# RWKV attention and a SiLU feed-forward on one core: the first chunk in pairs of neighbouring tokens, two batches per tile, its bonus summed on TensorE

## The chip, the cores and the metric

The kernel runs on 1 core of a Trainium2 chip. The metric is the device time of one execution in microseconds (us), lower is better. The kernel before has a median of 195.09 us over 3 runs (194.4, 195.09 and 197.38). About 2% is what a measurement of this kernel can tell from no change.

## What is computed

An RWKV-style linear attention with a per-channel decay, then a feed-forward layer with SiLU. Batch 4, 8 heads, 768 tokens, head size 48; model width 384, inner width 2048; 3072 tokens in all. Inputs and output are float32.

```python
def _attn_ref(r, k, v, w, u):
    state = np.zeros((B, H, D, D))
    for t in range(S):
        kt, vt, rt = k[:, :, t], v[:, :, t], r[:, :, t]
        cur = einsum('bhd,bhe->bhde', u[None] * kt, vt)
        y[:, :, t] = einsum('bhd,bhde->bhe', rt, state + cur)
        state = w[None, :, :, None] * state + einsum('bhd,bhe->bhde', kt, vt)

def _moe_ref(x, w_in, w_out):      # x: y with the heads side by side, 3072 x 384
    h = x @ w_in
    return (h * (1 / (1 + exp(-h)))) @ w_out
```

The term with `u` is the bonus: the token's own value, weighted by the sum over a head's channels of r * u * k.

## The kernel before

**Units and chunks.** Tokens are cut into 6 chunks of 128 (`C`). A unit is one chunk of one batch, so there are 24 units; unit i is chunk i // 4 of batch i % 4. Units 0 to 3 are the first chunk, which has no state coming in and whose decay runs over all 128 tokens. Later chunks are worked off in halves of 64 tokens (`HC`) and in pairs of batches.

**One unit of the first chunk.** r, k and v come in by one DMA each (`ld`, L72), one token per partition, so each contiguous piece is one token of one head, 48 floats or 192 bytes. In SBUF a head of r and k has 64 columns, of which 16 are zero. TensorE turns r and k (`turn_one`, L261): 8 transposes each, one for each pair of heads and each half of 64 tokens. All of them have 64 rows and 112 columns; the page writes such a shape as 64*112. VectorE multiplies what comes out by powers of w (`decay_one`, L269) into rT and kT. TensorE forms the products k.r of all pairs of tokens (`product_pair`, L295), VectorE masks them (`masked`, L302), TensorE multiplies them with v in half precision (`outputs_y`, L312), and VectorE adds the bonus while it copies the result out (`evict_y`, L317). Three transposes (`turn_y`, L469) and a copy on ScalarE (`copy_x`, L473) make it the input xT of the feed-forward. GpSimd does the bonus: k*u (L221), times r (L225); VectorE sums each head (L234); GpSimd multiplies v by that sum (`vu`, L239). GpSimd also makes the decayed k (`kc`, L229), from which `first_sums` (L326) and `first_state` (L337, L342) make the state that goes into the second chunk.

**The feed-forward.** `l1_mm` (L484) multiplies xT with 128 or 256 columns of `w_in` into PSUM, `l1_silu` (L492) applies SiLU on ScalarE, `l2_mm` (L505) multiplies with `w_out`, and `store` (L511 to L515) writes out. The weights come in by GpSimd's queue in four pieces each (`ld_win` L83, `ld_wout` L88), and are cast to half precision on the way.

**What sets the order.** Nothing is scheduled by a planner: each engine runs its instructions in the order in which the program emits them. From the first chunk to the middle of the second this order is a list of words written out by hand (`order`, L584 to L595). `T0` is the turning of unit 0, `rT0` its decay, `A01` the products of units 0 and 1, `am0` the mask, `Y0` the outputs, `y160` the bonus and copy, `yT0` and `xT0` the way to the feed-forward, `S0` and `st0` the states of units 0 and 1; `L0.4` and `G0.4` are `l1_mm` and `l1_silu` for the first two batches and columns 4 and 5 of 16, `L2.x` the same for the other two batches; `i_q1` asks for the second quarter of `w_in`. `4*` ahead of a word puts four 128x512 matmuls on zeros before it (`spin`, L166). `lnwb` and `lamC` (`powers_c`, L193 to L201) make the powers of w on ScalarE and load the SiLU table; `pads` (L160) zeroes the unused columns of eight input tiles on ScalarE. The PSUM tiles `att` alternate between two buffers; all others share four (tag "moe").

**Queues.** SyncE issues almost all loads; ScalarE issues the load of k for unit 0, of `u_bc` and of `w_row`. From `L2.0` on (L589) the order is the same in both kernels, but for the places of the two pair-wise steps named below.

Of the kernel before, what the change touches and what calls it, by code (L numbers as in the profile page):

```python
# [8 lines left out]
FP = mybir.dt.float32  # L9
# [6 lines left out]
def kernel(  # L16
# [11 lines left out]
    nc = tc.nc  # L28
# [33 lines left out]
    rin = [big.tile([128, H, 64], FP, name=f"rin{i}") for i in range(NIN)]  # L62
    kin = [big.tile([128, H, 64], FP, name=f"kin{i}") for i in range(NIN)]
    vin = [big.tile([128, H, D], FP, name=f"vin{i}") for i in range(NIN)]
    kc = [big.tile([128, H, 64], F16, name=f"kc{i}") for i in range(NIN)]
    st = [big.tile([PR, 2, NP, D], FP, name=f"st{b}") for b in range(B // 2)]
    win = big.tile([128, NQ, DFF], F16)
    wout = big.tile([128, NFT, HD], F16)

    def ld(i, dst, src, eng=nc.sync):  # L70
        sc, b = unit(i)
        eng.dma_start(  # L72
            out=dst[i % NIN][:, :, 0:D],
            in_=src[b, :, sc * C:sc * C + C, :].rearrange("h t d -> t h d"))

# [16 lines left out]
    def columns(eng, dst, src, j):  # L92
# [8 lines left out]
    nc.vector.memset(idle, 0.0)  # L101
    columns(nc.sync, wpT, w, 1)
    columns(nc.scalar, wpT, w, 0)
    nc.scalar.dma_start(out=w_row, in_=bass.AP(tensor=w.tensor, offset=0, ap=[[0, 1], [1, HD]]))
    ld(0, rin, r)
    ld(0, kin, k, nc.scalar)
    nc.scalar.dma_start(out=u_bc, in_=bass.AP(tensor=u.tensor, offset=0,
                                              ap=[[0, 128], [D, H], [1, D]]))
    ld(1, rin, r)
    ld(1, kin, k)  # L110
    ld(0, vin, v)
    ld(1, vin, v)
    load(2)
    load(3)
    nc.vector.memset(ones, 1.0)
    for i in range(B):
        nc.vector.memset(rin[i][:, :, D:64], 0.0)
        nc.vector.memset(kin[i][:, :, D:64], 0.0)
# [6 lines left out]
    it_rev = cst.tile([128, 1], FP)  # L125
    nc.gpsimd.iota(it_rev, pattern=[[0, 1]], base=C - 1, channel_multiplier=-1,
                   allow_small_or_imprecise_dtypes=True)
    it_half = cst.tile([128, 1], FP)
    for y in range(2):
        nc.gpsimd.iota(it_half[HC * y:HC * y + HC], pattern=[[0, 1]], base=HC - 1,  # L130
                       channel_multiplier=-1, allow_small_or_imprecise_dtypes=True)
    maskM = cst.tile([128, C], FP)
    nc.gpsimd.memset(maskM, 1.0)
    nc.gpsimd.affine_select(
        out=maskM, in_=maskM, compare_op=ALU.is_ge, fill=0.0,
        base=-1, channel_multiplier=-1, pattern=[[1, C]])
    ident16 = cst.tile([128, 128], F16)
    nc.gpsimd.tensor_copy(out=ident16, in_=ident)
    maskX = cst.tile([128, C], FP)
    maskH = cst.tile([128, HC], FP)  # L140
# [4 lines left out]
    for i in range(NIN):  # L145
        nc.gpsimd.memset(kc[i][:, :, D:64], 0.0)
# [6 lines left out]
    lamC = cst.tile([128, H, D], FP)  # L153
# [41 lines left out]
    def powers_c():  # L195
        nc.scalar.activation(out=lamC.rearrange("p h d -> p (h d)"), in_=lnw_bc,
                             func=AF.Exp, scale=it_rev)
# [4 lines left out]

    def cross_mask():
        nc.scalar.copy(out=maskX[0:HC, :], in_=maskM[HC:C, :])
        nc.scalar.copy(out=maskX[HC:C, :], in_=maskM[0:HC, :])
        for y in range(2):
            nc.scalar.copy(out=maskH[HC * y:HC * y + HC, :],
                           in_=maskM[HC * y:HC * y + HC, HC * y:HC * y + HC])
# [19 lines left out]
    def decayed_k(i):  # L228
        nc.gpsimd.tensor_tensor(out=kc[i % NIN][:, :, 0:D], in0=kin[i % NIN][:, :, 0:D],  # L229
                                in1=lamH if unit(i)[0] else lamC, op=ALU.mult)  # L230
# [33 lines left out]
    def decay_one(i, x):  # L264
        key, lam = (("rT", lamR), ("kT", lamK))[x]
        L(i)[key] = wrk.tile([PR, NP, C], FP, name=key)
        lam = (lam[:, :, 0:HC].unsqueeze(1).broadcast_to([PR, 2, NP, HC]) if unit(i)[0]
               else lam.rearrange("p g (y t) -> p y g t", y=2))
# [16 lines left out]
    def product_pair(i):  # L285
        a = [next_att().rearrange("p j (g c) -> p j g c", g=NP) for _ in range(2)]
        for e in range(2):
            L(i + e)["a"] = a[e]
# [397 lines left out]
```

## Time and profile before

One profiled execution took 194.21 us, with a span of 192.5 us; the remaining 1.7 us lie around the span.

| engine | busy, share of the span | busy from 0 to 25.48 us | busy from 50 us on (142.5 us) |
|---|---|---|---|
| TensorE (PE) | 180.4 us, 94% | 21.03 us | 136.99 us |
| VectorE (DVE) | 107.7 us, 56% | 18.15 us | 72.06 us |
| ScalarE (ACT) | 118.5 us, 62% | 17.03 us | 81.83 us |
| GpSimd (POOL) | 117.2 us, 61% | 20.76 us | 74.79 us |

25.48 us is where the first matmul of `L2.0` starts, the first step from which both kernels run the same list. The sixteen DMA engines are fully used in the first 50 us and at about half after that. Granted TensorE clock: 1.00 throughout. A profile's row of the timeline reads: start, length, engine, line, operation, written tile <- read tiles, shape (for TensorE: rows*columns of the stationary operand, then the moving one), how often, and in brackets the idle time ahead of it with what ended it. Rows of equal instructions in a run are merged; the length is from the start of the first to the end of the last.

### The profile page before, as it was taken

How to read it: one execution, taken by the hardware profiler on the slowest of the kernel's cores; microseconds unless marked ns; L12 is line 12 of the kernel's file. 1: busy time of each engine (PE TensorE's matmuls, PEld its weight loads, DVE VectorE, ACT ScalarE, POOL GpSimd, SP SyncE). 2: the span in 40 equal slices, each digit the busy share in tenths (PEclk: the TensorE clock that was granted, in tenths of full speed). 3: DMA queues.
4: the chain of work that ended last, by engine and by line, in shares of the span. 5: the costliest groups of instructions: out<-in, count | busy, mean ns of one | idle time of the engine just before them, and what ended most of it. 6: DMA issues, size and time to landing. Idle time of an engine off the chain costs nothing. (4 is left out here: it accounts for less than half of the span.)

```text
span 192.5 us, 6544 instructions
## 1 busy us (share of the span) xinstructions
PE 180.4 (94%) x2786; PEld 112.2 (58%) x2786; DVE 107.7 (56%) x183; ACT 118.5 (62%) x235; POOL 117.2 (61%) x151
## 2 busy tenths in 40 slices
PE   7888898989999999999999999999999999899993
PEld 2455684567756876745546646557656456444562
DVE  7578775846965846836827826917924914200120
ACT  5499478779383495198593297683397773189200
POOL 6499999599899955949659459469339320000000
PEclk9999999999999999999999999999999999999999
DMA  5999999999268568278185286294286201210022
GB/s 94 215 214 198 208 200 184 159 224 217 33 117 166 184 138 169 80 149 202 29 169 136 72 178 168 46 191 125 55 166 170 41 23 66 71 52 0 2 83 83
DMA packets 90272, 24.42 MB, mean 127 GB/s; under 512 B 83329, under 2 KB 90242, under 8 KB 90242
## 3 DMA queue, kind: packets, MB, share of 16 engines
q1 hardware_dynamic: 84992, 20.39, 48.4%
q0 software_dynamic: 3712, 3.15, 10.8%
q10 hardware_dynamic: 1538, 0.46, 1.1%
q8 instruction: 22, 0.36, 0.8%
q14 instruction: 8, 0.07, 0.1%
HBM read 20.65 MB, written 4.72 MB: 132 GB/s over the span
## 5 line engine op out<-in xcount | busy, mean ns | idle before, releaser
L484 PE MATMUL hps<-xT,win 128*128 128x512 f16 (+1 forms) x360 | 66.4, 337 | 1.0 <-DMA xT<-y 0.9
L492 ACT ACTIVATE gT<-hps 128x512 f16<-128x512 f32 x96 | 55.3, 600 | 16.6 <-PE hps L484 14.1
L505 PE MATMUL ops<-wout,gT 128*128 128x384 f16 x368 | 63.0, 326 | 1.3 <-ACT gT L492 1.3
L505 PEld LDWEIGHTS <-gT 128*128 128x128 f16 x368 | 34.9, 98 | 25.4 <-ACT gT L492 2.5
L484 PEld LDWEIGHTS <-win 128*128 128x128 f16 x360 | 33.6, 98 | 26.9 <-issue 2.1
L221 POOL TENSOR_TENSOR ku<-kin,u_bc 128x384 f32<-128x384 f32 x24 | 24.7, 1029 | 15.0 <-DMA kin<-in_k_dram 11.7
L239 POOL TENSOR_TENSOR vu<-vin,rku 128x384 f32<-128x384 f32 x24 | 19.8, 837 | 19.1 <-DVE rku L234 19.1
L511 ACT COPY osb<-ops 128x384 f32<-128x384 f32 x20 | 9.6, 478 | 30.7 <-PE ops L505 27.9
L448 DVE TENSOR_TENSOR y<-yp,vu 64x384 f16<-64x384 f32 x40 | 21.3, 554 | 11.8 <-PE yp L437 5.7
L225 POOL TENSOR_TENSOR rku_f<-rin,ku 128x384 f32<-128x384 f32 x24 | 24.5, 1020 | 1.7
L392 DVE TENSOR_TENSOR s<-sp,sdec 112x384 f32<-112x384 f32 x10 | 5.6, 558 | 32.9 <-PE sp L379 30.9
L229 POOL TENSOR_TENSOR kc<-kin,lamH 128x384 f16<-128x384 f32 x20 | 20.7, 1036 | 0.0
L269 DVE TENSOR_TENSOR kT<-att,lamK 112x512 f32<-112x512 f32 x24 | 16.3, 677 | 4.7 <-PE att L261 4.7
L269 DVE TENSOR_TENSOR rT<-att,lamR 112x512 f32<-112x512 f32 x24 | 16.2, 677 | 2.3 <-PE att L261 2.3
L337 ACT CAST s1h<-s 48x384 f16<-48x384 f32 x20 | 10.2, 510 | 6.5 <-DVE s L392 6.2
L248 ACT CAST v<-vin 128x384 f16<-128x384 f32 x24 | 11.5, 510 | 2.7 <-DMA vin<-in_v_dram 2.5
L513 DVE COPY osb<-ops 128x384 f32<-128x384 f32 x3 | 1.7, 558 | 20.5 <-issue 16.4
L234 DVE TENSOR_REDUCE rku<-rku_f 128x8 f32<-128x384 f32 x24 | 12.4, 538 | 1.0 <-POOL rku_f L225 1.0
L363 DVE TENSOR_TENSOR am<-att,maskH 128x1024 f16<-128x1024 f32 x10 | 12.2, 1218 | 1.3 <-PE att L356 1.3
L283 ACT CAST rT<-rT 112x512 f16<-112x512 f32 x20 | 12.4, 620 | 0.1
L356 PE MATMUL att<-rT,kT 48*64 48x64 f32 x640 | 11.6, 220 | 0.0
L356 PEld LDWEIGHTS att<-rT,kT 48*64 48x64 f32 x640 | 10.4, 135 | 0.0
(81 smaller groups left out, 183.8 us busy)
## 6 DMA issues: line engine op xcount, KB each, us to landing
rin<-in_r_dram SPq DMA_DIRECT2D x24, 192.0 KB, 3.6
vin<-in_v_dram SPq DMA_DIRECT2D x24, 192.0 KB, 4.7
kin<-in_k_dram SPq DMA_DIRECT2D x23, 192.0 KB, 4.7
out_dram<-osb SPq DMA_DIRECT2D x23, 192.0 KB, 3.2
win<-in_moe_w_in_dram POOLq DMA_DIRECT2D x4, 384.0 KB, 6.0
wout<-in_moe_w_out_dram POOLq DMA_DIRECT2D x4, 384.0 KB, 6.4
xT<-y SPq DMA_TRANSPOSE x18, 2.3
kin<-in_k_dram ACTq DMA_DIRECT2D x1, 192.0 KB, 3.8
```

The costliest lines, as they stand in the source:

```text
L221: nc.gpsimd.tensor_tensor(out=L(i)["ku"], in0=kin[i % NIN][:, :, 0:D], in1=u_bc, op=ALU.mult)
L225: nc.gpsimd.tensor_tensor(out=L(i)["rku_f"], in0=rin[i % NIN][:, :, 0:D], in1=L(i)["ku"], op=ALU.mult)
L229: nc.gpsimd.tensor_tensor(out=kc[i % NIN][:, :, 0:D], in0=kin[i % NIN][:, :, 0:D], in1=lamH if unit(i)[0] else lamC, op=ALU.mult)
L234: nc.vector.tensor_reduce(out=L(i)["rku"], in_=L(i)["rku_f"], axis=mybir.AxisListType.X, op=ALU.add)
L239: nc.gpsimd.tensor_tensor(out=L(i)["vu"], in0=vin[i % NIN], in1=L(i)["rku"].unsqueeze(2).broadcast_to([128, H, D]), op=ALU.mult)
L269: nc.vector.tensor_tensor(out=L(i)[key].rearrange("p g (y t) -> p y g t", y=2), in0=L(i)["t"][0:PR, :, x], in1=lam, op=ALU.mult)
L283: nc.scalar.copy(out=L(i)["rT16"], in_=L(i)["rT"])
L356: nc.tensor.matmul(a[o0:o0 + HC, j, e, p, :], kT[r0:r0 + D, p, HC * x:HC * x + HC], rT[r0:r0 + D, p, HC * x:HC * x + HC], start=True, stop ...
L448: nc.vector.tensor_tensor(out=L(i + e)["y16"][rows].rearrange("p h d -> p (h d)"), in0=L(i)["y2"][r][rows, 0:HD], in1=L(i + e)["vu"][rows] ...
L484: nc.tensor.matmul(hps[:, f, :], win[:, q, (ft + f) * 128:(ft + f + 1) * 128], xts[sc][:, q, b0:b0 + nb, :].rearrange("p b t -> p (b t)"), ...
L492: nc.scalar.activation(out=gts[sc][:, ft:ft + m, b0 * C:(b0 + nb) * C], in_=hpss[b0, ft], func=AF.Silu)
L505: nc.tensor.matmul(opss[b], gts[sc][:, ft, b * C:(b + 1) * C], wout[:, ft, :], start=(ft == 0), stop=(ft == NFT - 1))
```

## The change

Only the first chunk (units 0 to 3) is done in another way. Two batches become a pair (g = 0, 1); e names the batch in the pair, j the parity of a token.

- **Loads.** `ldX` puts batch 2g on partitions 0 to 63 and batch 2g+1 on 64 to 127. A partition holds tokens 2p and 2p+1, next to each other, so that a contiguous piece has 384 bytes. One DMA fills 64 partitions; there are as many DMAs as before and half as many pieces. A head now takes 112 columns (`DP`): 96 of data and 16 of padding. ScalarE issues both loads of k for pair 0 before `w_row`, and two small loads of u, transposed; `u_bc` moves to SyncE, behind the loads of pair 1.
- **Turning.** `turn_x` does one head at a time and one parity: for each pair of heads, first two transposes of 64*112 for the odd head, then two of 64*64 for the even one (each for the two batches). That is 32 for r and 32 for k of a pair of batches, where there were 16 and 16. In the program a 64*112 transpose has the tile size 64x128, a 64*64 one has 64x64.
- **Products by parity.** `product_x` does for each parity of k the two parities of r, 64x64 each; `masked_x` masks; `outputs_x` sums over the parity of k in PSUM, 64 small matmuls for a pair of batches.
- **Bonus.** GpSimd multiplies the decayed rT and kT (`bonus_x`); eight float32 matmuls with the factors u*w (`usel`) sum the heads on TensorE (`bonus_sum_x`); ScalarE copies the 16 sums per row (`bonus_out_x`); GpSimd multiplies v by them, as before. Per unit, two GpSimd products and a VectorE sum become one GpSimd product.
- **The rest.** The decayed k of a pair is one GpSimd instruction on 768 columns, and needs the powers `lamX` (two instructions in place of `lamC`). The masks are made on GpSimd; `cross_mask` and the two swapped copies of v go for the first chunk. The state is made in six smaller copies per pair in place of three (`state_x`).
- **The order.** The list is written anew up to `L2.0`. Of what follows, only `x.S.1` and `x.st.1` stand where `S2` and `st2` stood, and the steps `kc2`, `kc3` and `i_q3` are elsewhere.

```diff
+    def ldX(g, dst, src, eng=nc.sync):
+        for e in range(2):
+            o = dst[g][HC * e:HC * e + HC]
+            o = o.rearrange("p h j d -> p h (j d)") if dst is vX else o[:, :, 0:2 * D]
+            eng.dma_start(out=o, in_=src[2 * g + e, :, 0:C, :].rearrange(
+                "h (p j) d -> p h (j d)", j=2))
...
     columns(nc.sync, wpT, w, 1)
     columns(nc.scalar, wpT, w, 0)
+    ldX(0, rX, r)
+    ldX(0, kX, k, nc.scalar)
     nc.scalar.dma_start(out=w_row, in_=bass.AP(tensor=w.tensor, offset=0, ap=[[0, 1], [1, HD]]))
...
-    load(2)
-    load(3)
+    ldX(0, vX, v)
+    columns(nc.scalar, uT, u, 0)
+    columns(nc.scalar, uT, u, 1)
+    ldX(1, rX, r)
+    ldX(1, kX, k)
+    ldX(1, vX, v)
...
     def powers_c():
-        nc.scalar.activation(out=lamC.rearrange("p h d -> p (h d)"), in_=lnw_bc,
-                             func=AF.Exp, scale=it_rev)
+        for j in range(2):
+            nc.scalar.activation(out=lamX[:, :, j, :],
+                                 in_=lnw_bc.rearrange("p (h d) -> p h d", h=H),
+                                 func=AF.Exp, scale=it_two[:, j:j + 1])
...
+    def turn_x(g, x):
+        t = X(g)["t", x] = next_att().rearrange("p e (j g t) -> p e j g t", j=2, g=NP)
+        src = (rX, kX)[x][g].rearrange("p h x -> p (h x)")
+        for j in range(2):
+            for p in range(NP):
+                for h, p0, n in ((2 * p + 1, 64, PR), (2 * p, 0, 64)):
+                    for e in range(2):
+                        rows = slice(HC * e, HC * e + HC)
+                        c0 = DP * h + D * j - p0
+                        nc.tensor.transpose(t[0:n, e, j, p, :], src[rows, c0:c0 + n],
+                                            ident[rows, rows])
...
+    def bonus_sum_x(g):
+        bk = X(g)["bk"] = ps.tile([128, 512], FP, name="bk", tag="moe", bufs=4)
+        for j in range(2):
+            for p in range(NP):
+                c0 = 2 * (NP * j + p)
+                nc.tensor.matmul(bk[:, c0:c0 + 2], X(g)["q", j][:, p, :], usel[:, p, :],
+                                 start=True, stop=True)
...
     order = """
-        lnw eK lamK mx clear lr4 lk4 lv4 lr5 lk5 lv5 lr6 lk6 lv6 lr7 lk7 lv7 4*T0 ku0 rT0 kT0
-        4*T1 rT1 kT1 v160 ru0 rd0 ku1 wb v161 A01 ru1 am0 rd1 vu0 lnwb i_q0 lamC pads am1 vu1
-        4*Y0 y160 T2 kT2 2*Y1 y161 ku2 ru2 rT2 yT0 xT0 i_q1 yT1 xT1 v162 T3 kT3 rT3 ku3 ru3 rd2
-        v163 4*A23 vu2 i_q2 rd3 vu3 am2 am3 L0.0 G0.0 L0.2 G0.2 Y2 y162 Y3 y163 kc0 yT2 xT2 L0.4
-        G0.4 kc1 yT3 xT3 L0.6 G0.6 S0 st0 kc2 T4 kT4 rT4 kc3 L2.0 G2.0 L2.2 G2.2 ku4 v164
-        L2.4 G2.4 S2 L2.6 G2.6 st2 ru4 i_q3 r164 L4.8 G4.8 L4.9 G4.9 rd4 ku5 kc4 kc5 sd4
+        lnw eK lamK us clear lr4 lk4 lv4 lr5 lk5 lv5 lr6 lk6 lv6 lr7 lk7 lv7
+        4*x.t.0.0 x.d.0.0.0 x.d.0.0.1 x.t.0.1 x.d.0.1.0 x.d.0.1.1 x.q.0.0 x.q.0.1 i_q0
+        2*wb lnwb x.P.0.0 x.P.0.1 x.m.0.0 x.m.0.1 lamX x.v16.0 pads x.B.0 x.rk.0 x.vu.0.0 x.vu.0.1 i_q1
+        x.t.1.0 x.d.1.0.0 x.d.1.0.1 x.t.1.1 x.d.1.1.0 x.d.1.1.1 2*x.Y.0 x.e.0.0 x.e.0.1
+        x.q.1.0 x.q.1.1 i_q2 2*x.yT.0 x.xT.0.0 x.xT.0.1 x.P.1.0 x.m.1.0 x.P.1.1 x.m.1.1 x.v16.1
+        L0.0 G0.0 L0.2 G0.2 x.B.1 x.rk.1 x.vu.1.0 x.vu.1.1 L0.4 G0.4 x.kc.0 i_q3 x.Y.1 x.e.1.0 x.e.1.1
+        L0.6 G0.6 x.yT.1 x.xT.1.0 x.xT.1.1 x.S.0 x.st.0 x.kc.1 T4 kT4 rT4
+        L2.0 G2.0 L2.2 G2.2 ku4 v164 L2.4 G2.4 x.S.1 L2.6 G2.6 x.st.1 ru4 r164 L4.8 G4.8 L4.9 G4.9
```

In the new words, `x.t.g.0` turns r of pair g and `x.t.g.1` its k; `x.d` are the decays, `x.q` the GpSimd products for the bonus, `x.B` their sums on TensorE, `x.rk` the copy of the sums, `x.vu` v times the sums, `x.P` the products, `x.m` the masks, `x.Y` the outputs, `x.e` the bonus and copy, `x.yT` and `x.xT` the way to the feed-forward, `x.kc` the decayed k, `x.S` and `x.st` the state.

## The prediction

> **What bounds the kernel now.** I read the page's first two parts, then busy time by stage, then the timelines of TensorE and ScalarE up to 26 us, then DMA. The first view is the page; the second gives busy time in three stages (length, then each engine, then clock, DMA share, GB/s).
>
> ```profile
> PE 180.4 (94%) x2786; PEld 112.2 (58%) x2786; DVE 107.7 (56%) x183; ACT 118.5 (62%) x235; POOL 117.2 (61%) x151
> ...
> DMA  5999999999268568278185286294286201210022
> ```
> ```profile
> 0.00:25.48 25.48, 21.03 (x316) 12.88 (x317) 18.15 (x38) 17.03 (x40) 20.76 (x41) 1.00 1.02 188
> 25.48:50.00 24.52, 22.36 (x450) 15.58 (x450) 17.48 (x30) 19.68 (x38) 21.65 (x25) 1.00 1.09 186
> 50.00:192.50 142.50, 136.99 (x2044) 83.74 (x2036) 72.06 (x117) 81.83 (x157) 74.79 (x86) 1.00 0.46 106
> ```
>
> From 50 us on TensorE is busy for 136.99 of 142.5 us: nothing done earlier elsewhere shortens that. The change edits only what stands ahead of the first matmul of L2.0. So the question is one number: when does L2.0 start, now 25.48 us? The list behind it is the same, so a delay there passes to the end nearly one for one. From 25.48 to 50 us TensorE idles 24.52 - 22.36 = 2.2 us, mostly behind engines fed by TensorE itself, so I let that move along and absorb nothing.
>
> TensorE's timeline around a turn (line 261) shows what a new shape of the array costs; the last line, from the tile's own view, has min/median/max ns of one transpose:
>
> ```profile
> 12.86 0.37 PE L312 MATMUL yp<-v,am 128*128 128x48 f16 x8 [0.36 <-DVE am L302]
> 13.16 0.44 PE L261 MATMUL att<-ident,rin 64*112 64x64 f32 x8
> 13.43 0.39 PE L261 MATMUL att<-ident,kin 64*112 64x64 f32 x8
> 13.75 0.60 PE L166 MATMUL zs<-idle 128*128 128x512 f16 x2
> ...
> 25.48 2.14 PE L484 MATMUL hps<-xT,win 128*128 128x256 f16 x18
> ```
> ```profile
> L261 PE MATMUL att<-ident,kin x48: 216/216/269, 5.9 to 31.1; 64*112 64x64 f32 x48
> ```
>
> Eight transposes run as four pairs (two row halves at once). In the second run the last pair starts 0.39 - 0.216 = 0.17 us after the first: 0.058 a pair, 0.23 for four. But the first run takes 0.27 until the second starts, so entering the shape cost 0.04, and the second takes 0.32 until the spin starts, so leaving cost 0.09. A change of shape is 0.13 us, over twice the pair itself. Before, a unit pays it once for 16 transposes.
>
> ScalarE's timeline has the chain that the new bonus must go through; DMA's has two stretches of the SyncE queue (packets, MB, share of sixteen engines), from 10 to 12 us with 192-byte pieces, and from 63 to 64 us almost all 1536-byte rows:
>
> ```profile
> 11.45 0.49 ACT L193 ACTIVATE lnw_bc<-bc 128x384 f32<-128x384 f32 x1
> 11.97 0.61 ACT L196 ACTIVATE lamC<-lnw_bc,it_rev 128x384 f32<-128x384 f32 x1
> 12.49 0.60 ACT L198 ACTIVATE lamH<-lnw_bc,it_half 128x384 f32<-128x384 f32 x1
> 13.00 0.19 ACT L200 ACTIVATE wHT<-lnwT 112x4 f32<-112x4 f32 x1
> 13.20 1.28 ACT L201 ACT_TABLE_LOAD   x1
> 14.50 0.30 ACT L160 CAST rin<-idle 128x128 f32<-128x128 f16 x1
> ```
> ```profile
> q1 hardware_dynamic: 2229, 0.42, 107.3%
> ```
> ```profile
> q1 hardware_dynamic: 301, 0.39, 105.4%
> ```
>
> **Part 1, loads (gain).** 1.073 x 16 x 2 us / 2229 = 15.4 ns for 192 bytes. In the other stretch 50 of the 301 packets are under 512 bytes and nearly free, so 1.054 x 16 us / 251 = 67 ns for 1536. The straight line gives 23 ns for 384 bytes, against 31 for two of 192. Before, the second k landed when its transposes began, at 8.15 us. Now pair 0 needs r and k, 128 packets an engine, 2.9 us; the first r load before landed 3.0 us after its issue at 1.43, of which 1.0 was its own 64 packets, so the flow counts from about 3.2 and pair 0 is there at 5.9 to 6.1 us; I take 5.9. The two added loads of u on ScalarE cost its queue 0.43 us each, and delay the powers of w (3.26 us now) by one to two us; the first decay comes after 9, which hides it.
>
> **Part 2, turning (loss).** `turn_x` alternates 64*112 and 64*64 pairs, 16 pairs a call. If every pair pays the change, one costs 0.058 + 0.13 = 0.19 to 0.2 us, so a call lasts 3.2 us against 16 x 0.058 = 0.93. Bounds: 0.058 (the change of width is free; below that nothing speaks for a gain) and 0.266 a pair (each waits for all of the one before, the longest record). I take 0.2, because changes of shape cost about that everywhere in this timeline. [...]
>
> **Part 3, the chain with these prices (us).** TensorE: r of pair 0 5.9 to 9.1, its k to 12.3. VectorE's two k decays (0.6 each) end at 13.1 and 13.75. TensorE: two spins 0.5 and `wb` 0.85, to 13.65 (row of before: 8.52 to 9.36); products 2 x 0.55 to 14.75 (64 of this shape take 1.16 at 33.34). GpSimd: `q` twice from 13.1; 384 columns take 1.0, so 512 take 1.3: 15.7, then `i_q0` 0.8. ScalarE from 13.75: 0.5 + 3 x 0.52 + 0.2 + 1.3 for `lnwb`, powers and table, two casts 1.0, eight pads 0.2 each, together 6.15 = 19.9; only then, in its own order, the copy of the bonus sums, 20.1. `vu` twice (0.82) on GpSimd ends at 21.75, and `i_q1`, queued behind it, is issued there; it took 6.0 to land, so 27.75.
>
> TensorE meanwhile: bonus sums 15.7 to 16.4 (8 float32 matmuls; bounds 0.3 by the transposes' rate and 1.1 by a 0.13 us weight load each; both stay inside waits), then, in order ahead of `x.Y.0`, the two turns of pair 1: 16.4 to 22.8. Spins 0.5, outputs 0.6: 23.9. VectorE: last decays of pair 1 to 24.15, `x.e` to 25.25. TensorE: y transposes to 25.65, products of pair 1 to 26.75; ScalarE's two copies 26.7; L0.0 and L0.2 at 0.75 each, 28.25; sums 28.95; L0.4 (weights there) 29.7; `x.Y.1` 30.3. The bonus of pair 1: ScalarE copy 29.25, `vu` twice 30.95; `x.e.1.1` 31.5; transposes 31.9; ScalarE 32.9; GpSimd's `x.kc.0` (768 columns, 1.9) ends at 32.85; state matmuls 33.35; T4 33.9. So L2.0 starts at 33.9 instead of 25.48: 8.4 us late.
>
> GpSimd drops about 2.7 us of chunk-0 work (3.8 a unit now; then 1.3 + 0.82 + 0.95), and the swapped copies (2.0 us on ScalarE), mask copies and four VectorE sums (2.2) go. I cost these at nothing: all three engines wait for TensorE here. The six state copies (0.36 against 0.56 for half the columns) lie beside L2.x.
>
> **Sum:** 194.2 (profiled execution) + 8.4 = 202.6 us. The median of before stands 0.9 above the profiled execution; I keep the latter. The 2% (what a measurement can tell) end at 191.2 and 199.0.
>
> [...]
>
> **The rivals.**
> - *The change of width is free; not slower.* At 0.058 a pair: r and k turned at 7.8, `wb` 9.15, copy of the sums after ScalarE's 6.15 at 15.6, `vu` 17.25, `i_q1` lands at 23.25, L0.4 24.0, `x.Y.1` 24.6, `x.e` 25.75, ScalarE 27.05, L2.0 27.4: +1.9, 196.1 us, no change. For it: no row of before alternates 64*112 with 64*64. Against it: every other change of shape in the timeline leaves such a gap. It decides from about 0.08 us a change down (a pair at 0.13 gives +4.7).
> - *The loads win.* Pair 0 is there 2.2 us earlier, and nothing behind it takes longer: 192 us. Against it, ScalarE's order puts table and pads ahead of the copy.
> - *The clock drops as well.* Spins step by 0.48 us in the first 5 us (4 in 1.9) and by 0.26 later (4 in 1.04). If the long stretches of tiny matmuls count as idle, two turns at half speed add 2 x 3.2 x 0.85 = 5.4: 208. Against it: granted clock 1.00 in all stages.
> - *The pieces don't get cheaper:* +1.0 us, inside the forecast's range.
>
> **How the numbers follow.** Forecast 0.72, free change 0.15, clock 0.09, loads win 0.04. The forecast's own range is 200 (a pair at 0.15, +5.7) to 206.8 (a pair at 0.266: 4 x 16 x 0.066 = 4.2 more). The range for 8 in 10 takes in the free change: 196.1 to 206.8. Slower by over 2%: forecast and clock, less a little for short changes, 0.78; within 2%: 0.19; faster: 0.03.
>
> **What would show it.** Right: the first matmul of the second half's l1 near 34 us; each call of the turn about 3.2 us with starts of pairs 0.2 apart; a wait of GpSimd's `vu` for ScalarE from about 16.5 to 20 us. Wrong: pairs 0.06 apart, or L2.0 before 29 us. Pair 0's transposes should start near 5.9; if at 7 or later, the price of a 384-byte packet is wrong. If TensorE idles less than 2.2 us between L2.0 and 25 us later, part of the delay was absorbed, which I have ruled out.

## The result, and the profile after

The changed kernel takes 209.32 us (median of 4 runs, 208.34 to 211.23); the kernel before took 195.94 us beside it (194.4 to 197.38). The ratio is 1.072 with a 95% interval of 1.059 to 1.086: slower by 13.4 us. (A ratio leaves out executions more than 1.5% above the fastest of their kernel and a median keeps them, so the two need not agree to the last digit.) The direction was forecast; the time lies above the forecast of 202.6 and above the range.

The profiled execution took 211.23 us, the slowest of the four, with a span of 209.5 us. That is 17.0 us above the profiled execution of before (194.21), so the trace holds 3.6 us more loss than the medians. First the page, then three stages cut as before, at the first matmul of L2.0, now 41.00 us, and 24.52 us later.

```profile
PE 191.8 (92%) x3130; PEld 123.5 (59%) x3130; DVE 105.5 (50%) x185; ACT 116.3 (56%) x230; POOL 115.2 (55%) x148
...
PEclk9999797699999999999999999999999999999999
DMA  5999999394982395793982966929929511120022
```
```profile
0.00:41.00 41.00, 32.20 (x645) 23.98 (x645) 16.92 (x36) 14.80 (x35) 17.91 (x38) 0.88 1.00 157
41.00:65.52 24.52, 22.43 (x474) 15.59 (x472) 18.00 (x34) 19.68 (x38) 22.05 (x25) 1.00 0.82 122
65.52:209.50 143.98, 137.21 (x2040) 83.94 (x2026) 70.61 (x116) 81.84 (x157) 75.20 (x86) 1.00 0.59 105
```

The loss sits where the prediction looked for it. L2.0 starts 15.5 us later; the stage behind it is as busy as before (22.43 us against 22.36) and the rest is 1.5 us longer. What fills the 15.5 us is another matter. TensorE leaves twice as many records ahead of L2.0, is at work for 11.2 us more, idles 4.35 us more, and its granted clock is 0.88. TensorE's timeline of the changed kernel:

```profile
6.26 0.32 PE L321 MATMUL att<-ident,rin 64*112 64x64 f32 x1 [1.38 <-DMA rin<-in_r_dram]
8.31 1.85 PE L321 MATMUL att<-ident,rin 64*112 64x64 f32 x30 [1.73 <-DMA rin<-in_r_dram]
...
10.02 1.95 PE L321 MATMUL att<-ident,kin 64*64 64x64 f32 x31
...
13.99 2.10 PE L375 MATMUL att<-rT,kT 48*64 48x64 f32 x128
16.02 1.95 PE L350 MATMUL bk<-usel,q 112*128 112x2 f32 x16
17.89 0.27 PE L321 MATMUL att<-ident,rin 64*112 64x64 f32 x2
19.87 1.45 PE L321 MATMUL att<-ident,rin 64*64 64x64 f32 x30 [1.71 <-issue]
...
26.44 1.97 PE L375 MATMUL att<-rT,kT 48*64 48x64 f32 x119
30.87 0.49 PE L375 MATMUL att<-rT,kT 48*64 48x64 f32 x9 [2.45 <-issue]
31.29 2.74 PE L604 MATMUL hps<-xT,win 128*128 128x256 f16 x12
33.83 1.92 PE L350 MATMUL bk<-usel,q 112*128 112x2 f32 x16
...
41.00 1.26 PE L604 MATMUL hps<-xT,win 128*128 128x256 f16 x10
```

Four things stand here that the prediction had not. The second half of r lands at 8.3 us, not at 5.9. A transpose lasts 311 ns where it lasted 216, and the twelve matmuls of L0.0 and L0.2 take 2.74 us where they took 1.49: TensorE runs at half its clock. (The clock's first record in this trace, of full clock, is at 13.48 us; the view shows full clock ahead of it too, though the lengths say half: the transposes of k from 21.11 us, inside a recorded half stretch, last 311 ns as well. From there on the records have half clock in three stretches of 3.41 us, from 20.31, 30.55 and 37.38.) Products and bonus sums take about 2 us a call. And twice TensorE stands still for 1.7 and 2.5 us inside a run of equal matmuls, with no releaser ("issue").

ScalarE, and then GpSimd, up to the second quarter of the weights:

```profile
20.14 0.16 ACT L355 COPY rkux<-bk 128x16 f32<-128x16 f32 x1
```
```profile
20.39 1.61 POOL L359 TENSOR_TENSOR vu<-vin,rkux 128x384 f32<-128x384 f32 x2 [4.11 <-ACT rkux L355]
21.95 0.80 POOL L100 DMA_DIRECT2D win<-in_moe_w_in_dram  x1
```

This chain came within 0.2 us of the forecast (20.1, 21.75), in part by luck: the loads came 2.4 us late, and the two turns, 3.66 us together, were 2.7 us shorter than the forecast's 6.4. SyncE's queue from 10 to 12 us, the stretch shown of before:

```profile
q1 hardware_dynamic: 986, 0.37, 127.8%
```

1.278 x 16 x 2 us / 986 = 41.5 ns for 384 bytes, where 192 took 15.4: the larger pieces go slower, 0.37 MB against 0.42 MB in the same time.

### The profile page after: what moved, and what is told of

Read it like the earlier page. It is cut to its first block, busy times and chain, and to the rows that moved or that the text cites. A ratio compares the mean times of both kernels' runs of the same rounds, so it can differ in the third digit from the quotient of the medians.

```text
span 209.5 us, 7225 instructions
## 1 busy us (share of the span) xinstructions
PE 191.8 (92%) x3130; PEld 123.5 (59%) x3130; DVE 105.5 (50%) x185; ACT 116.3 (56%) x230; POOL 115.2 (55%) x148
## 4 chain that ended last, share of the span: by engine, by line
PE 76%; ACT 10%; DMA 5%; issue 4%; DVE 2%; SPq 1%; DVEq 0%; ACTq 0%
PE hps L604 26%; PE ops L625 25%; PE att L286 4%; ACT gT L612 4%; PE att L475 4%; PE att L321 3%; DMA rin<-in_r_dram 3%; DMA out_dram<-osb 2%; PE att L375 2%; PE yp L548 2%; ACT v L273 2%; PE bk L350 2%; PE yp L557 2%; PE sp L499 2%; PE ops L650 1%
## 5 line engine op out<-in xcount | busy, mean ns | idle before, releaser
L604 PE MATMUL hps<-xT,win 128*128 128x512 f16 (+1 forms) x360 | 68.3, 344 | 1.3 <-PE ops L625 0.9
L604 PEld LDWEIGHTS <-win 128*128 128x128 f16 x360 | 34.4, 100 | 28.0 <-issue 2.3
L246 POOL TENSOR_TENSOR ku<-kin,u_bc 128x384 f32<-128x384 f32 x20 | 20.1, 1004 | 16.5 <-DMA kin<-in_k_dram 16.2
L264 POOL TENSOR_TENSOR vu<-vin,rku 128x384 f32<-128x384 f32 x20 | 16.5, 840 | 14.7 <-DVE rku L259 14.7
L250 POOL TENSOR_TENSOR rku_f<-rin,ku 128x384 f32<-128x384 f32 x20 | 20.9, 1045 | 1.4
L293 DVE TENSOR_TENSOR kT<-att,lamK 112x512 f32<-112x512 f32 x20 | 13.5, 676 | 3.8 <-PE att L286 3.8
L293 DVE TENSOR_TENSOR rT<-att,lamR 112x512 f32<-112x512 f32 x20 | 13.5, 674 | 0.0
L483 DVE TENSOR_TENSOR am<-att,mk 128x1024 f16<-128x1024 f32 x10 | 12.2, 1217 | 1.3 <-PE att L475 1.3
L359 POOL TENSOR_TENSOR vu<-vin,rkux 128x384 f32<-128x384 f32 x4 | 3.2, 819 | 13.0 <-ACT rkux L355 13.0
L259 DVE TENSOR_REDUCE rku<-rku_f 128x8 f32<-128x384 f32 x20 | 10.1, 534 | 0.0
```

The source lines that it names most:

```text
L246: nc.gpsimd.tensor_tensor(out=L(i)["ku"], in0=kin[i % NIN][:, :, 0:D], in1=u_bc, op=ALU.mult)
L250: nc.gpsimd.tensor_tensor(out=L(i)["rku_f"], in0=rin[i % NIN][:, :, 0:D], in1=L(i)["ku"], op=ALU.mult)
L264: nc.gpsimd.tensor_tensor(out=L(i)["vu"], in0=vin[i % NIN], in1=L(i)["rku"].unsqueeze(2).broadcast_to([128, H, D]), op=ALU.mult)
L293: nc.vector.tensor_tensor(out=L(i)[key].rearrange("p g (y t) -> p y g t", y=2), in0=L(i)["t"][0:PR, :, x], in1=lam, op=ALU.mult)
L483: nc.vector.tensor_tensor(out=am.rearrange("p j e g c -> p (j e g) c"), in0=L(i)["a2"].rearrange("p j e g c -> p (j e g) c"), in1=maskH.un ...
L604: nc.tensor.matmul(hps[:, f, :], win[:, q, (ft + f) * 128:(ft + f + 1) * 128], xts[sc][:, q, b0:b0 + nb, :].rearrange("p b t -> p (b t)"), ...
```

## The experiments

"Ratio" is always to the kernel before on the same chip, with its 95% interval; the changed kernel's is 1.072.

**1. Widths grouped** (the forecast's own theory). The 64*112 transposes of a call first, then the 64*64:

```diff
-        for j in range(2):
-            for p in range(NP):
-                for h, p0, n in ((2 * p + 1, 64, PR), (2 * p, 0, 64)):
+        for i, p0, n in ((1, 64, PR), (0, 0, 64)):
+            for j in range(2):
+                for p in range(NP):
+                    h = 2 * p + i
```

> Changed kernel, but each turn does its sixteen transposes of 64*112 first and its sixteen of 64*64 after them, so the width changes once a call instead of 15 times. My theory of the prediction (a change of width costs 0.13 us): 4 x 14 x 0.13 = 7 us less, about 202 us. Rival, read from the changed kernel's trace (a turn of 32 takes 1.45 to 1.95 us, so a change of width is nearly free): 209.3 us, within 0.5.

Measured: 211.87 us, ratio 1.087 [1.078, 1.096]. Its two turns of the first pair:

```profile
8.45 1.95 PE L322 MATMUL att<-ident,rin 64*112 64x64 f32 x31 [1.69 <-DMA rin<-in_r_dram]
10.10 2.01 PE L322 MATMUL att<-ident,kin 64*112 64x64 f32 x32
```

A call has 16 pairs. With one change of width in it instead of 15 its turn lasts as long, 1.95 and 2.01 us against 1.85 and 1.95, at the same half clock. Changing the width costs nothing here; the theory falls.

**2. Opposite halves.** ScalarE's two loads of k in reverse order, so that the queues fill different partition halves at a time.

```diff
-        for e in range(2):
+        for e in ((0, 1) if eng is nc.sync else (1, 0)):
```

> Changed kernel, but ScalarE issues the two loads of k of pair 0 in the reverse order, so that SyncE's stream and ScalarE's fill opposite partition halves at any time. Theory of the halves (a load into 64 partitions runs at about half rate because sixteen DMA engines write into one half): r and k of pair 0 are there about 2 us earlier (first full turn at 6.3 instead of 8.3 us), 384-byte packets at 25 ns instead of 40, and 2 us or more off the total, about 207. Rival (384-byte pieces are slow as such): no change of either.

Measured: 210.83 us, ratio 1.076 [1.067, 1.086]. No gain: r can be turned in full at 8.60 us (8.31 in the changed kernel). That both queues fill the same half is not what slows them.

**3. The kernel before with its spins in eight pieces each**, 252 instructions more:

```diff
-            nc.tensor.matmul(zs, idle[:, 0:128], idle, start=True, stop=True)
+            for c in range(0, 512, 64):
+                nc.tensor.matmul(zs[:, c:c + 64], idle[:, 0:128], idle[:, c:c + 64],
+                                 start=True, stop=True)
```

> Kernel before, but each 128x512 matmul of the spins is cut into eight of 128x64: the same TensorE time, 252 more instructions on TensorE's list in the first 18 us. Theory of the instruction fetch (TensorE's two idle stretches of 1.7 and 2.5 us in the changed kernel, 512 instructions apart and released by nothing, are waits for its own instructions): one or two such stretches of 1 to 2.5 us appear, total 197 to 200 us. Rival (they come from something else in the changed kernel): 195.9 us, no such stretch.

Measured: 198.51 us, ratio 1.014 [1.006, 1.023]. No wait without a releaser of 1 us or more. TensorE waited 1.31 us for r of unit 1, and ran at half clock from 8.7 to 15.6 us:

```profile
9.27 0.68 PE L263 MATMUL att<-ident,rin 64*112 64x64 f32 x8 [1.31 <-DMA rin<-in_r_dram]
```

So 252 more instructions alone, at this rate, make no such wait. What the trace shows in the place of one is late data and half clock; that these two make up the 3 us was not tested by itself.

**4. The kernel before with half loads.** Loads of the first chunk by two units and 64 partitions, 192-byte pieces as before:

```diff
-    ld(0, rin, r)
-    ld(0, kin, k, nc.scalar)
+    ldH(0, rin_all, r)
+    ldH(0, kin_all, k, nc.scalar)
...
+    def ldH(g, dst, src, eng=nc.sync):
+        for y in range(2):
+            eng.dma_start(
+                out=dst[HC * y:HC * y + HC, 2 * g:2 * g + 2, :, 0:D],
+                in_=src[2 * g:2 * g + 2, :, HC * y:HC * y + HC, :].rearrange(
+                    "i h t d -> t i h d"))
```

> Kernel before, but the loads of the first chunk go by pairs of units and halves of partitions: as many DMAs, the same 192-byte pieces, 192 KB each into 64 partitions. Theory of the halves: packets of the first 8 us take about 25 ns instead of 15.4, the four loads of r and k of units 0 and 1 are there 2 us later, total 197.5 to 199.5 us. Rival (only the piece size matters): 15.4 ns, total within 1 us of 195.9 (unit 0 then waits for four DMAs instead of two).

Measured: 198.78 us, ratio 1.018 [1.011, 1.025]. The time is inside the theory's range, but not for its reason. Below are SyncE's queue (q1) and ScalarE's (q10) from 4 to 8 us, two rows each: before, this kernel, the changed kernel.

```profile
q1 hardware_dynamic: 2869, 0.54, 69.1%
q10 hardware_dynamic: 806, 0.32, 35.1%
q1 hardware_dynamic: 2329, 0.44, 66.4%
q10 hardware_dynamic: 2120, 0.45, 64.5%
q1 hardware_dynamic: 1485, 0.56, 93.2%
q10 hardware_dynamic: 758, 0.21, 41.3%
```

A packet of SyncE's took 0.664 x 16 x 4 us / 2329 = 18.2 ns here, not the theory's 25, and both queues together moved 0.89 MB, where before moved 0.86. In the changed kernel the same sum gives 40.2 ns, and 0.77 MB were moved. So with 192-byte pieces the 64 partitions cost no throughput. The four loads of units 0 and 1 are there at 8.55 us, against 8.0 before; but unit 0 now waits for all four (r can be turned in full at 7.04), where before it waited for its own two, which landed at 4.4 and 5.8. TensorE idled 2.3 of the 3.41 us up to 7.42, and from there to 17.7 us the clock was half.

**5. New products in bfloat16.** Decayed r and k, q and the factors of the first chunk; half the records for each matmul, less exact.

```diff
-        t = X(g)[key, j] = wrk.tile([PR, NP, C], FP, name=key)
+        t = X(g)[key, j] = wrk.tile([PR, NP, C], BF, name=key + "b")
...
-        X(g)["q", j] = wrk.tile([PR, NP, C], FP, name="q")
+        X(g)["q", j] = wrk.tile([PR, NP, C], BF, name="q")
...
-    usel = cst.tile([PR, NP, 2], FP)
+    usel = cst.tile([PR, NP, 2], BF)
```

> The changed kernel, with the decayed r and k of the first chunk, their products for the bonus and the bonus factors in bfloat16 instead of float32 (so these are less exact; nothing else differs). x.P.0 has then 64 records of TensorE instead of 128, x.B.0 8 instead of 16, with as many weight loads fewer: some 290 records fewer before L2.0. Theory that the float32 matmuls of P and B are mis-sized in my sum and that TensorE waits for its own instructions: P goes from 2.1 to 1.0 us, B from 1.95 to under 1, the two idles without a releaser (at records 449 and 961) shrink to under 0.5 us or stand at the same counts, thus at other matmuls; in all 3 to 6 us less, 204 to 206. Rival, the late loads and the half clock alone: P and B get shorter, but the engine then waits for VectorE and GpSimd in their place, and the time stays above 207.

Measured: 203.26 us, ratio 1.040 [1.033, 1.046]: 6.1 us less. `x.P.0` takes 0.71 us, `x.B.0` 0.25 a half. One wait without a releaser is left, of 0.74 us, and L0.4 waits 2.2 us for its weights, which land at 28.4.

```profile
14.04 0.71 PE L376 MATMUL att<-rTb,kTb 48*64 48x64 bf16 x64
...
24.40 0.19 PE L376 MATMUL att<-rTb,kTb 48*64 48x64 bf16 x1 [0.74 <-issue]
```

Between the changed kernel's profile and this one products and sums themselves shrink by 6.0 us, and the waits without a releaser from 4.16 to 0.74 us; of these 9.4 us 6.1 reached the end, since new waits (for the weights, and 0.55 us for q) took up a part.

**6. Sixteen spins instead of four** ahead of the first turn, to keep TensorE at work until r is there.

```diff
-        4*x.t.0.0 x.d.0.0.0
+        16*x.t.0.0 x.d.0.0.0
```

> The changed kernel, with 16 spins instead of 4 ahead of the first turn, so that TensorE stays at work until both halves of r have landed at 8.3 us. Theory that the half clock is caused by TensorE's idle time ahead (here 4.9 to 8.3) and costs what it looks like: the first two turns take 1.0 us each instead of 1.85, wb and the products follow at full speed, L2.0 starts 2 to 3 us earlier, 206 to 207.5; the later half windows stay, because the idles at records 449 and 961 stay. Rival, that the granted clock is not what sets the pace of these small matmuls: the turns take 1.85 us at a clock of 1.00, and the time stays at 209 within 1.

Measured: 205.35 us, ratio 1.048 [1.038, 1.057]: 4.0 us less by medians, 4.8 by ratios, by doing more. The median holds the profiled execution at 211.09 us, which has three waits without a releaser (0.84, 1.42 and 1.67 us) and half clock again from 28.45 to 38.69 us; the other three took 203.61 to 206.03. The first turn is now at full clock:

```profile
8.54 1.05 PE L321 MATMUL att<-ident,rin 64*112 64x64 f32 x30 [0.97 <-DMA rin<-in_r_dram]
```

**7. The same with each spin in four pieces**, to move the count of instructions and nothing else.

```diff
-            nc.tensor.matmul(zs, idle[:, 0:128], idle, start=True, stop=True)
+            for c in range(0, 512, 128):
+                nc.tensor.matmul(zs[:, c:c + 128], idle[:, 0:128], idle[:, c:c + 128],
+                                 start=True, stop=True)
```

> As the run with 16 spins, but every spin of 512 columns is cut into four of 128 (also those elsewhere in the kernel): the same columns in four times as many instructions, 96 records more ahead of the first turn. Theory that TensorE waits for its own instructions, whose stretches end at records 449, 961 and 1473: idles without a releaser are again found at these counts, thus some 100 records earlier in the list (the first within x.P.0 or x.B.0 in place of the first turn of pair 1). Rival, that the idles belong to the place (the first turn of pair 1, the products of pair 1): they stay at those lines, at counts some 100 higher. The time says little here; within 2 of the run with 16 whole spins.

Measured: 205.22 us, ratio 1.042 [1.031, 1.053]. Here are the counts. Each row below is cut in the middle of a wait without a releaser; the two numbers in brackets after PE and PEld are the records up to there or since the last one. First the changed kernel, then this one, then run 9:

```profile
0.00:19.50 19.50, 13.77 (x222) 9.20 (x222) 9.11 (x23) 8.57 (x20) 7.35 (x27) 1.00 1.11 167
19.50:30.50 11.00, 8.30 (x255) 6.44 (x256) 4.82 (x7) 2.62 (x9) 5.62 (x6) 0.84 1.04 168
```
```profile
0.00:24.20 24.20, 21.30 (x477) 18.37 (x478) 12.62 (x29) 10.99 (x28) 12.97 (x33) 0.93 1.09 172
24.20:30.20 6.00, 5.51 (x128) 4.96 (x127) 2.36 (x2) 2.16 (x5) 1.03 (x2) 1.00 1.14 200
```
```profile
0.00:22.50 22.50, 17.95 (x349) 11.19 (x350) 13.17 (x30) 10.34 (x27) 11.46 (x32) 0.92 1.06 164
```

The waits stand at 444 and 955 records, at 955 and 1210, and at 699. All are 444 plus a multiple of 255 or 256, whatever the matmul: in the changed kernel 444 falls into the first turn of pair 1, and 955 after 119 of the 128 records of `x.P.1`; here 955 falls after 41 of them, and 1210 into `x.Y.1`. Runs 1 and 11 have theirs at 444 and 955 too, run 5 at 699. Not every such count has a wait: the changed kernel passes 699 without one. The wait goes with the count of records and not with a place in the computation:

```profile
24.26 1.51 PE L377 MATMUL att<-rT,kT 48*64 48x64 f32 x87 [0.94 <-issue]
...
30.34 1.09 PE L408 MATMUL yp<-v,am 64*64 64x48 f16 x57 [0.57 <-issue]
```

**8. Half loads in the kernel before, with 14 spins** instead of 4 ahead of the first turn.

```diff
-        4*T0 ku0 rT0 kT0
+        14*T0 ku0 rT0 kT0
```

> The kernel before, with the first chunk's loads cut by partition halves over two units (as in the earlier run, 198.8 us), and 14 spins instead of 4 ahead of the first turn, to bridge the later landing. Theory that most of those 3.5 us came through the clock (half from 7.4 to 17.7): the clock stays at 1.00 and the time falls to 196 to 197. Rival, that the lateness of the loads alone makes it: 198 to 199 again.

Measured: 197.30 us, ratio 1.011 [1.002, 1.021], clock 1.00 from 5.7 us on. Of the 3.5 us that half loads cost, an estimate by medians puts about 1.5 on the clock and about 2 on the lateness, which includes unit 0's wait for the loads of two units; the two intervals overlap.

**9. Both remedies** (the edits of 5 and 6).

```diff
-        t = X(g)[key, j] = wrk.tile([PR, NP, C], FP, name=key)
+        t = X(g)[key, j] = wrk.tile([PR, NP, C], BF, name=key + "b")
...
-        4*x.t.0.0 x.d.0.0.0
+        16*x.t.0.0 x.d.0.0.0
```

> The changed kernel with both edits: bfloat16 for the new products and bonus sums (less exact), and 16 spins ahead of the first turn. Theory that the loss is a sum of late loads, half clock and TensorE's wait for its instructions, each with a remedy of its own: the clock stays at 1.00 from 5 us, the first turns take 1.05 us, x.P.0 begins at 11.8 instead of 14.0, L2.0 starts at 30.5 to 31.5 instead of 33.0, and the time is 200.5 to 202. Rival, that the wait of L0.4 for the second quarter of the weights (2.2 us in the bfloat16 run) is the bound: ScalarE's list begins 2.2 us earlier as well, thus the rival says the same gain, but with that wait still at 2 us or longer; and a third, that the two remedies remove the same loss: 203 again.

Measured: 200.10 us, ratio 1.020 [1.012, 1.027]: 9.2 us of the 13.4 are gone, nearly the sum of the two (10.1).

```profile
8.46 1.05 PE L322 MATMUL att<-ident,rin 64*112 64x64 f32 x30 [0.88 <-DMA rin<-in_r_dram]
...
11.76 0.89 PE L376 MATMUL att<-rTb,kTb 48*64 48x64 bf16 x64
13.46 0.25 PE L351 MATMUL bk<-usel,q 112*128 112x2 bf16 x4 [0.81 <-POOL q L342]
14.57 0.25 PE L351 MATMUL bk<-usel,q 112*128 112x2 bf16 x4 [0.86 <-POOL q L342]
14.75 1.93 PE L322 MATMUL att<-ident,rin 64*112 64x64 f32 x32
...
22.62 0.29 PE L376 MATMUL att<-rTb,kTb 48*64 48x64 bf16 x13 [0.59 <-issue]
...
29.53 2.14 PE L605 MATMUL hps<-xT,win 128*128 128x256 f16 x18
```

The turn of 32 transposes takes 1.05 us at full clock (0.066 us a pair, the lower bound of the forecast), and 1.93 where the clock drops again, behind the two waits for GpSimd's q. The time is 0.4 us below the theory's range, although the clock did not stay full: it was half from 14.81 to 18.23 us.

**10. Run 9 with the bonus copy early**: sums and ScalarE's copy ahead of powers, table, casts and pads.

```diff
-        x.m.0.0 x.m.0.1 lamX x.v16.0 pads x.B.0 x.rk.0 x.vu.0.0
+        x.m.0.0 x.m.0.1 x.B.0 x.rk.0 lamX x.v16.0 pads x.vu.0.0
```

> As the run with bfloat16 and 16 spins, with the bonus sums of the first pair and ScalarE's copy of them moved ahead of ScalarE's powers, table load, casts and pads. Theory that with TensorE quick again the chain ScalarE copy, vu on GpSimd, issue of the second quarter of the weights is what sets L0.4: the copy comes at 13 to 14 us instead of 18, the issue at 16, the wait of L0.4 for its weights goes, and L2.0 starts 2 to 3 us earlier, 198 to 199.5 us. Rival: the weights are late through the traffic and not through the issue, or TensorE has something else to wait for; within 1 us of the run without the move.

Measured: 200.14 us, ratio 1.021 [1.014, 1.027]: nothing. The chain did get shorter, and the wait moved to the next thing GpSimd owes, the decayed k ahead of the state matmuls:

```profile
15.44 1.62 POOL L360 TENSOR_TENSOR vu<-vin,rkux 128x384 f32<-128x384 f32 x2
17.01 0.80 POOL L101 DMA_DIRECT2D win<-in_moe_w_in_dram  x1
```
```profile
29.25 0.45 PE L444 MATMUL sp<-v,kc 64*64 64x48 f16 x32 [0.77 <-POOL kc L433]
```

**11. Only that move in the changed kernel** (the edit of 10, float32, 4 spins).

```diff
-        lamX x.v16.0 pads x.B.0 x.rk.0
+        x.B.0 x.rk.0 lamX x.v16.0 pads
```

> The changed kernel with only that move (bonus sums and ScalarE's copy ahead of powers, table, casts and pads; float32, 4 spins). My prediction had the copy at 20.1, vu at 21.75 and the issue of weights there, which all came true. Theory that TensorE was later than that chain all the same, so that moving it brings nothing: 208.5 to 210, within 1 of the changed kernel, with GpSimd's wait of 4.1 us gone. Rival, that this chain was part of the loss: 206 to 207.

Measured: 208.27 us, ratio 1.062 [1.052, 1.072]. The two intervals overlap; a gain of about 1 us can't be told from none. Its profiled execution, at 207.07 us, has L2.0 at 36.72 us, a second wait without a releaser of 0.65 us instead of 2.45, and one stretch of half clock instead of three: so much of the 41.00 us above belongs to the one execution that was profiled.

**12. The kernel before with bfloat16 products** (less exact).

```diff
-        L(i)[key] = wrk.tile([PR, NP, C], FP, name=key)
+        L(i)[key] = (wrk.tile([PR, NP, C], FP, name=key) if unit(i)[0]
+                    else wrk.tile([PR, NP, C], BF, name=key + "b"))
```

> The kernel before, with the decayed r and k of the first chunk in bfloat16 (less exact), so that the products of the first chunk leave half the records. Theory that bfloat16 gains 6 us in the changed kernel because it takes away a wait for instructions and the half clock behind it, and the before has neither: 0 to 1 us less, 194.4 to 195.4. Rival, that it is simply TensorE time in both: 192 or less.

Measured: 195.27 us, ratio 1.000 [0.997, 1.004]. What gains 6 us in the changed kernel gains nothing here.

```profile
8.35 0.67 PE L262 MATMUL att<-ident,rin 64*112 64x64 f32 x8
```

But the profiled execution was at half clock up to 17.29 us (that of before up to 5.52), with L2.0 at 26.21 us instead of 25.48. So the run doesn't show what the halving by itself is worth: a gain may have gone into the clock.

**13 to 15. The order, once more.** These three have the edits of 9, and the outputs behind L2.0 turned by TensorE and copied by ScalarE instead of by a DMA. The first is their base; the second turns pair 1 ahead of the bonus sums; the third also asks for the first two quarters of the weights ahead of q and vu.

```diff
-        turn_y_dma(i)
-        turn_y_dma(i + 1)
+        for n in (i, i + 1):
+            turn_y(n)
+            copy_x(n)
...
-        x.v16.0 pads x.B.0 x.rk.0 x.vu.0.0 x.vu.0.1 i_q1
-        x.t.1.0 x.d.1.0.0 x.d.1.0.1 x.t.1.1 x.d.1.1.0 x.d.1.1.1 2*x.Y.0
+        x.v16.0 x.t.1.0 x.d.1.0.0 x.d.1.0.1 x.t.1.1 x.d.1.1.0 x.d.1.1.1
+        x.B.0 x.rk.0 pads x.vu.0.0 x.vu.0.1 i_q1 2*x.Y.0
```

> As the run with bfloat16 and 16 spins (200.1 us), but from the second half on the outputs y are turned by TensorE and copied by ScalarE, as those of the first chunks are, and not by a DMA. That lies behind L2.0 and serves only as the base for the next two kernels, which have it too. TensorE gets 60 transposes more, about 0.1 us each, on the path: 203 to 208 us; L2.0 at 29.5 to 30.5 as before.

> As its base, with the turns and decays of the second pair ahead of the bonus sums of the first, the copy of the sums ahead of the pads. In the run with bfloat16 and 16 spins TensorE waited 1.7 us for GpSimd's q between 12.5 and 14.6 us, and the clock was half from 14.8 to 18.2, under the two turns. Theory that this is part of the 4.7 us that remain: TensorE turns while q is made, outputs of the first pair begin at 17.0 to 17.5 instead of 18.8, L2.0 at 27.5 to 28.5, and the time is 1 to 2 us below the base. Rival, that the 4.7 us are the late first loads (8.5 us instead of 5.8 before, about 2 us by the run with half loads and spins) and the larger number of instructions, and the order has nothing more to give: within 0.6 us of the base, the gain at the outputs lost again ahead of L2.0.

> As the run with the turns ahead of the sums, and the first two quarters of the weights asked for ahead of GpSimd's q and vu instead of behind them (2.2 and 1.6 us earlier). Theory that the second quarter then sets L0.4: a further 0.5 to 1.5 us less. Rival, that the transfers are full already and earlier weights take the place of loads of r, k and v: no less, within 0.7 of the run without that move.

Measured: 213.54, 215.09 and 213.62 us, ratios 1.094 [1.088, 1.101], 1.097 [1.088, 1.106] and 1.092 [1.084, 1.100] (of the second kernel one execution of 1030 us, the profiled one, is left out of the ratio). No difference. In the third kernel's profiled execution the outputs did begin at 17.06 us and L2.0 at 28.72, against 19.23 and 30.52 in the base's, with a new wait without a releaser of 1.28 us at `x.P.1`; its median shows no gain. The base itself missed its expectation by more than 5 us, behind L2.0. From 30 us on TensorE is at work for 6.1 us more than in run 9, by the transposes it was given, and idles 6.9 us more, most of it waiting for VectorE's y ahead of them (what waits for what, us in total, times, longest; the base, then run 9):

```profile
PE yT L585 <- DVE y L569: 9.7, 19, 1.8
```
```profile
PE yT L590 <- DVE y L569: 0.6, 2, 0.3
```

So these runs don't tell what the last 4.7 us are made of.

## Why the prediction was wrong

**What held.** The loss arises ahead of L2.0 and passes to the end. GpSimd waits for ScalarE's copy as forecast, and `i_q1` is issued at 21.95 us (21.75 forecast).

**The step that failed is part 2.** "A change of shape is 0.13 us" was read off the ends of runs in the timeline, where a new operation with new operands begins, and laid on every alternation inside one operation. Run 1 takes 14 of the 15 changes of each call away and nothing gets shorter; run 9 has 0.066 us a pair. A turn takes 1.05 us at full clock, not 3.2. Two of the forecast's own signs of being wrong came with it: pairs 0.06 apart, and pair 0's transposes later than 7 us. By itself the right price would have given the rival "the change of width is free", 196.1 us. The trace had no row for the alternation, and the forecast took the nearest row for the price, not for a bound. A 64-wide float32 transpose is no slower than the others: in the changed kernel's trace the 64 transposes of k of both pairs, 32 of each width, all last 311 or 312 ns.

**Part 1 had the wrong sign.** The straight line from 15.4 ns for 192 bytes to 67 ns for 1536 gave 23 ns for 384; measured were 41.5. Pair 0 was complete at 8.3 us, not 5.9. The rest of that sum was right: 128 packets at 40 ns are 5.1 us, and from 3.2 they end at 8.3. (By the forecast's own rows the flow would start at 4.43 - 1.0 = 3.4, a slip of 0.2.) Before, the same four loads were complete at 8.0, but unit 0 could start with its own two, at 4.4 and 5.8; that pair 0 needs four was in the forecast, and only cheaper packets could have paid for it. Run 4's packets, 192 bytes into 64 partitions, took 18.2 ns, so the 64 partitions alone don't make the price. Whether it is the 384 bytes, or these together with the 64 partitions or with the padding of a head to 112 columns, was not tested. Half loads gained nothing in these runs; a loss of throughput by the halves alone they don't show (run 4: 0.89 MB against 0.86), and run 8's 2 us contain unit 0's wait for two units.

**The clock was dismissed by a wrong reading.** The rival "the clock drops as well", at 0.09, gave 208, nearest to the result. That nearness is luck: it took turns of 3.2 us and slowed them, for being made of tiny matmuls; what the runs show are turns of 1.05 us slowed behind an idle wait for loads. Against it stood "granted clock 1.00 in all stages". But that view has nothing ahead of the clock's first record, and the spins of before at 0.48 us in the first 5 us against 0.26 later, which the same rival quoted, were half clock by their length. In the changed kernel TensorE idles from 4.9 to 8.3 us but for one transpose, and stays at half speed to 13.5. Run 6 prices it: 4.0 us by medians, 4.8 by ratios. In the clock's records of the changed kernel the half stretches ahead of L2.0 last 3.41 us each. In the 3.41 us ahead of a drop TensorE idled 1.7 us in the changed kernel (the wait at 18.2 to 19.9, ahead of the drop at 20.31), 2.3 in run 4, and not at all in run 7 (15.6 us): how much idle time brings a drop these runs don't show.

**Two mis-sized terms.** Products: "2 x 0.55" came from 64 records in 1.16 us, read as 64 matmuls. A float32 matmul of the products leaves two records here; the 64 matmuls of the two calls leave 128, and take 2.10 us. (The float32 transposes leave one each, 32 a call.) Bonus sums: 0.7 forecast with an upper bound of 1.1; 1.95 measured, 0.12 us a record for two columns of output.

**One mechanism was missing.** TensorE stands still where nothing that the trace shows holds it. Products and sums put 144 matmul records, with as many weight loads, into 4 us, and at some of the counts 444 + 255 or 256 n it waits without a releaser, for 1.71 and 2.45 us in the changed kernel. Run 7 shows that the places go with the count. Run 5, with half the records for products and sums, loses only 0.74 us that way. That it waits there for the next part of its own list is a reading of the "instruction" queue, here from the changed kernel's page:

```profile
q8 instruction: 24, 0.39, 0.9%
```

These are 24 packets of 16 KB for 6,260 records of TensorE, 261 each. In the changed kernel two of them land at 18.12 and 29.41 us, and the matmuls go on at 19.87 and 30.87; in run 7 they land at 22.83 and 29.07, and the matmuls go on at 24.26 and 30.34. Fifteen such waits stand ahead of L2.0 in nine of the traces, and each ends 1.3 to 1.75 us after a packet has landed. At 699 the changed kernel comes later than that and doesn't wait: it passes at 24.86 us, a packet having landed at 22.62. Why a packet starts when it does was not tried, and run 3 had more instructions without such a wait.

**The sum.** 13.4 us, by medians: 4.0 go with the spins (half clock behind late loads), 5.2 more with bfloat16 (products and sums at half the records, waits without a releaser and half clock behind them), 4.7 remain (200.10 against 195.38 beside it; the three add to 13.9, since the medians come from different chip runs; by ratios they are 4.8, 5.5 and 3.8 of 14.1). Late loads may be about 2 of the remaining 4.7, an estimate by run 8; GpSimd's q with another half stretch is seen in run 9's rows, but runs 13 to 15 could not confirm it. The rest is open. The forecast reached 22.8 us for the end of pair 1's turns, and the trace has 22.96: turns that were too dear stood in for loads, clock, products, sums and waits that were too cheap. From there on nothing covered the errors, and L2.0 came 7.1 us after its forecast: in this trace mostly by the second wait without a releaser (2.45), the products of pair 1 (about 1.4 more than forecast), L0.0 and L0.2 at half clock (1.25 more) and the bonus sums (about 1.1 more).

## What to carry to other kernels

Read the pace of a stage from the length of a known instruction in that stage (a transpose: 216 ns before, 311 here) before trusting a clock column, and ask of every late load what TensorE does meanwhile: here it idled from 4.9 to 8.3 us but for one transpose and ran at half speed to 13.5, and twelve more spins there took 4.0 us off. Count records as well as microseconds: the 144 matmul records of a pair's products and sums, with as many weight loads, took 4 us here, and the waits without a releaser added 4.16. With half the records for products and sums, 6.0 us of matmul time and 3.4 us of waits left the profile, and 6.1 us reached the end. A price taken at the edge of a run of instructions is a bound, not a price, for what happens inside one; the cheapest experiment, regrouping, should come to mind when a forecast rests on it.

## What the runs showed that was not expected

- Fifteen waits without a releaser ahead of L2.0, at 444, 699, 955 and 1210 records of TensorE in nine kernels, 0.6 to 3.1 us long, each ending 1.3 to 1.75 us after a 16 KB packet of instructions has landed.
- A bridge of 12 more spins, 2.5 us of useless work in an idle stretch, takes 4.0 us off by medians, 4.8 by ratios.
- Run 7's clock was half from 15.6 to 19.0 us though TensorE had no gap in the 3.4 us ahead: 1.7 us of these were bonus sums, with two columns each. The third half stretch of the changed kernel (from 37.38) follows such sums too, but run 7's second sums (27.02 to 28.86) and run 11's (30.18 to 32.02) were followed by no drop. Whether such matmuls bring the drop is open.
- 384-byte packets into 64 partitions took 41.5 ns where 192-byte packets into 128 took 15.4, and 192-byte packets into 64 took 18.2 (run 4).
